# Delta attention and two Mlps in one kernel: two weight blocks converted later, and attention's list ordered by a table

## The chip, the cores and the metric

The kernel runs on one core of one Trainium2 chip. The metric is the device time of one execution in microseconds, the median of several; 1 us is 1000 ns. The engines are TensorE (PE in the rows; its weight loads are PEld), VectorE (DVE), ScalarE (ACT), GpSimd (POOL) and SyncE (SP), which issues most of the DMA transfers. Each engine works through its own instructions in the order in which the program lists them.

## The reference

Three stages, one after the other. Attention is a delta rule over 768 tokens for 32 (batch, head) pairs with 48 values each: a state that every token reads and updates. Its output, 3072 rows of 384, goes through two Mlps with 2048 hidden values; the first has a rational function between its two products, the second h * tanh(softplus(h)).

```python
for t in range(S):                       # 768 tokens, for all (batch, head) pairs
    y[:, :, t] = einsum('bhd,bhde->bhe', q[:, :, t], state)
    v_old = einsum('bhde,bhd->bhe', state, k_n[:, :, t])
    state = state + beta[:, :, t] * einsum('bhd,bhe->bhde', k_n[:, :, t], v[:, :, t] - v_old)

h = x @ moe_w_in                         # 3072 x 384 by 384 x 2048
g = (a0 + a1*h + a2*h**2 + a3*h**3) / (1 + |b0|*|h| + |b1|*h**2 + 1e-6)
x = g @ moe_w_out                        # 2048 x 384
h = x @ moe2_w_in
out = (h * tanh(log1p(exp(h)))) @ moe2_w_out
```

The weights of the Mlps come as 64-bit floats.

## The kernel before

**Attention** works in chunks of 64 tokens, twelve of them (u = 0 to 11), in class `Attention`. `prepare(u)` loads and normalizes k, transposes k and q on TensorE (line 383), copies them out on ScalarE (line 387), forms the Gram products (lines 398 and 419) and masks them on VectorE. `inverse(u)`, once for each pair of chunks, solves 32x32 triangular systems: a transpose on VectorE (line 534), then 30 short steps of a product and a sum each (lines 552 and 558) on GpSimd, or on VectorE for the pairs that end with u = 1 and u = 9 (`ON_DVE`), then a last product (line 580) and a transpose back into `xt` on VectorE (line 586). `step(u)` is the recurrence: products on TensorE (lines 690, 707, 728, 736 and 751), each evicted by ScalarE or VectorE before the next can start, from the state of chunk u to that of chunk u + 1. It needs the inverse of its pair (line 707 reads `xt`).

**The weights.** A product in full precision is made of three passes with a high and a low part of each operand, so each of the 16 blocks of 128 hidden values of each Mlp is converted from 64-bit floats first (class `Weights`). A block has two sides, w_in and w_out. One side is a raw load by SP, a scaling on ScalarE (`mag`, line 852), three bit operations on VectorE (`size`, `sign`, `low`; lines 856, 861, 867), a copy on ScalarE (`out`, line 874) and a difference on GpSimd (`rest`, line 879). All 16 blocks of the first Mlp are converted during attention: blocks 2 to 15 are stored to DRAM and fetched again when the first Mlp runs, blocks 0 and 1 stay. There the three bit operations keep their intermediate word in PSUM (`w1.word`); where that is not set, it lies in the raw block in SBUF.

**The order of attention.** `prepare`, `inverse`, `step`, the weights and the split of the first x group add every operation to a `Plan` with its engine, a duration written in the program, and the buffers that it reads and writes. `Plan.order` walks through time: whichever engine is free takes, of its operations that are ready, the one with the highest priority, which is the longest way to the end of the list (`tail`), less `early`, plus a bias of its kind (engine and first buffer written). For the weights `early` is 4000 ns times the block's place less 60000. `Plan.best` tries 2500 random changes of the biases and keeps those that don't lengthen the planned end; `Plan.run` issues the operations in that order and puts matmuls on zeros (`heat`, line 1239) into planned gaps of TensorE.

**The Mlps** run 96 units each: 6 groups of 512 tokens by 16 weight blocks. A unit is nine matmuls up (line 999), the function on ScalarE, VectorE and GpSimd, and nine matmuls down (line 1025) four units later. Each engine's order is written out in `MLP_OPS` and `FIRST_OPS` (the first four units). The up of unit i + 2 uses the PSUM bank that VectorE's second product of unit i (line 1090) frees. Ahead of unit 0 SP issues five weight fetches (`LOOK`, line 911), then one in each unit (`fw`).

**Conversions in the Mlps** go through class `Conv`: `start` issues three raw loads, `pull(n)` issues the next n of VectorE's steps and hands the ScalarE and GpSimd steps of a side to a list that the next unit's `f` empties; the first `mag` is issued at the first pull. Before, `Conv` holds the second Mlp's blocks alone. From unit `CONV_START` = 6 on, in units away from a new group (`calm`, 67 of them), it converts eight of them, 48 steps; the others in the second Mlp. In the list of a unit the pull, `c`, stands last.

```python
fetch_w = {n: (w1.fetch_split, FQ + LOOK + n) for n in range(NF - FQ - LOOK)}
calm = [i for i in range(CONV_START, n1 - 8) if not any(starts(i + 5 - k) for k in range(3))]
for f in range(LOOK):
    w1.fetch_split(FQ + f)
```

## Time and profile before

| what | us |
|---|---|
| median of 3 runs | 1092.06 |
| lowest and highest | 1089.65, 1092.43 |
| the profiled execution | 1098.82 |
| its span, first to last instruction | 1097.1 |
| TensorE busy in it | 1049.6 |
| VectorE, ScalarE, GpSimd busy | 686.7, 605.0, 553.0 |

The profile is one execution, and times in the rows are counted from the start of its span. An engine's busy time tells little by itself here, because matmuls on zeros count as busy. The views to read are the busy times by stage, the groups of instructions by line (with the idle time ahead of them and what ended it), and the instructions in order of time where one stage turns into the next. TensorE's granted clock stands in the windows as a share of 2.4 GHz.

### The profile page before, as it was taken

How to read it: one execution, taken by the hardware profiler on the slowest of the kernel's cores; microseconds unless marked ns; L12 is line 12 of the kernel's file. 1: busy time of each engine (PE TensorE's matmuls, PEld its weight loads, DVE VectorE, ACT ScalarE, POOL GpSimd, SP SyncE). 2: the span in 40 equal slices, each digit the busy share in tenths (PEclk: the TensorE clock that was granted, in tenths of full speed). 3: DMA queues.
4: the chain of work that ended last, by engine and by line, in shares of the span. 5: the costliest groups of instructions: out<-in, count | busy, mean ns of one | idle time of the engine just before them, and what ended most of it. 6: DMA issues, size and time to landing. Idle time of an engine off the chain costs nothing.

```text
span 1097.1 us, 24930 instructions
## 1 busy us (share of the span) xinstructions
PE 1049.6 (96%) x10228; PEld 895.5 (82%) x10228; DVE 686.7 (63%) x1154; ACT 605.0 (55%) x1081; POOL 553.0 (50%) x640
## 2 busy tenths in 40 slices
PE   7988889988889999999999999999999999999998
PEld 6988878877768888888888888888888888888897
DVE  6886658785369999999999999882222222222211
ACT  4534645324478888989889898643232322323222
POOL 4388998186268888787888888763000000000000
PEclk9998989889899999999999999999999999999999
DMA  8727875057691121211203046340101102011010
GB/s 127 139 63 182 223 201 138 10 152 218 220 362 70 39 78 43 84 47 73 87 15 104 13 144 245 101 145 1 28 30 15 43 2 57 1 22 36 10 20 29
DMA packets 152947, 99.25 MB, mean 90 GB/s; under 512 B 114048, under 2 KB 136192, under 8 KB 152832
## 3 DMA queue, kind: packets, MB, share of 16 engines
q1 hardware_dynamic: 150976, 96.77, 31.1%
q8 instruction: 80, 1.31, 0.5%
q10 hardware_dynamic: 1600, 0.79, 0.2%
q0 software_dynamic: 256, 0.10, 0.1%
q14 instruction: 35, 0.29, 0.1%
HBM read 66.16 MB, written 31.46 MB: 89 GB/s over the span
## 4 chain that ended last, share of the span: by engine, by line
PE 83%; DVE 7%; issue 3%; POOL 3%; ACT 1%; SPq 1%; DMA 1%; DVEq 0%; POOLq 0%; ACTq 0%
PE h L999 35%; PE o L1025 33%; PE o L1039 3%; PE c_ps L707 3%; PE y_ps L751 3%; DVE xraw L552 2%; PE c_ps L728 1%; PE c_ps L690 1%; PE t_ps L383 1%; SPq L252 1%; PE s_all L736 1%; DVE s_all L558 1%; POOL x L558 1%; PE t_ps L398 1%; DVE x L558 1%
## 5 line engine op out<-in xcount | busy, mean ns | idle before, releaser
L999 PE MATMUL h<-x,w 128*128 128x512 f32 x1728 | 426.4, 391 | 4.1 <-DVE s L1090 1.9
L1025 PE MATMUL o<-gh,w 128*128 128x512 f32 x1584 | 387.6, 389 | 0.0
L999 PEld LDWEIGHTS h<-x,w 128*128 128x128 f32 x1728 | 325.0, 188 | 73.8 <-DVE s L1090 3.0
L1025 PEld LDWEIGHTS o<-gh,w 128*128 128x128 f32 x1584 | 297.3, 188 | 61.7
L1121 ACT ACTIVATE gh<-h 128x512 fp32r<-128x512 f32 x96 | 57.5, 599 | 263.1 <-PE h L999 263.1
L1014 DVE TENSOR_TENSOR gh<-g,gh 128x512 fp32r<-128x512 f32 x80 | 55.0, 687 | 232.4 <-ACT g L1126 232.4
L1014 POOL TENSOR_TENSOR gh<-g,gh 128x512 fp32r<-128x512 f32 x112 | 145.4, 1299 | 67.4 <-ACT gh L1010 45.7
L1074 POOL TENSOR_TENSOR q<-q,r 128x512 f32<-128x512 f32 x96 | 131.8, 1373 | 29.9 <-ACT r L1068 25.1
L1088 DVE TENSOR_TENSOR s<-s,h 128x512 f32<-128x512 f32 x96 | 65.3, 681 | 27.7 <-ACT s L1070 17.0
L1070 ACT ACTIVATE s<-h,ab 128x512 f32<-128x512 f32 x96 | 74.0, 771 | 5.1 <-PE h L999 5.1
L1061 ACT ACTIVATE q<-h 128x512 f32<-128x512 f32 x96 | 57.5, 599 | 35.0 <-PE h L999 34.8
L1090 DVE SCALAR_TENSOR_TENSOR s<-s,ab,h 128x512 f32<-128x512 f32 x96 | 71.8, 748 | 3.4
L1101 DVE SCALAR_TENSOR_TENSOR r<-s,ab,r 128x512 f32<-128x512 f32 x96 | 71.8, 748 | 0.0
L1106 DVE SCALAR_TENSOR_TENSOR g<-q,r 128x512 f32<-128x512 f32 x96 | 66.0, 687 | 3.3
L1081 ACT ACTIVATE r<-q,cst 128x512 f32<-128x512 f32 x96 | 66.1, 688 | 1.7 <-POOL q L1074 1.7
L558 POOL TENSOR_TENSOR x<-x,xraw 128x30 f32<-128x30 f32 (+14 forms) x120 | 62.2, 518 | 9.4
L1097 DVE SCALAR_TENSOR_TENSOR q<-q,r 128x512 f32<-128x512 f32 x96 | 65.3, 680 | 0.9 <-ACT r L1083 0.6
L879 POOL TENSOR_TENSOR w<-wm,w 128x384 fp32r<-128x384 f32 x48 | 49.6, 1037 | 32.0 <-ACT w L874 23.7
L552 POOL TENSOR_TENSOR xraw<-x 128x30 f32<-128x30 f32 (+14 forms) x120 | 60.2, 502 | 7.3
L1010 ACT CAST gh<-g 128x512 fp32r<-128x512 f32 x96 | 59.1, 616 | 0.5 <-DVE g L1106 0.5
L1083 ACT ACTIVATE r<-r 128x512 f32<-128x512 f32 x96 | 55.9, 582 | 3.1
L1126 ACT ACTIVATE g<-h 128x512 f32<-128x512 f32 x96 | 57.0, 594 | 0.0
(139 smaller groups left out, 1283.5 us busy)
## 6 DMA issues: line engine op xcount, KB each, us to landing
w<-w SPq DMA_DIRECT2D x36, 768.0 KB, 6.9
w<-in_moe_w_in_dram SPq DMA_DIRECT2D x32, 384.0 KB, 3.7
w<-in_moe_w_out_dram SPq DMA_DIRECT2D x32, 384.0 KB, 3.6
xraw<-x SPq DMA_DIRECT2D x36, 256.0 KB, 4.1
w<-wt SPq DMA_DIRECT2D x8, 768.0 KB, 3.5
kn<-in_k_dram SPq DMA_DIRECT2D x48, 96.0 KB, 3.8
qn<-in_q_dram SPq DMA_DIRECT2D x48, 96.0 KB, 4.2
v<-in_v_dram SPq DMA_DIRECT2D x48, 96.0 KB, 3.4
```

The costliest lines, as they stand in the source:

```text
L552: eng.tensor_tensor(out=tv, in0=ls[:, j, j + 1:HC].unsqueeze(1).to_broadcast([128, j, n]), in1=xs[:, 0:j, j:j + 1].to_broadcast([128, j, n ...
L558: eng.tensor_tensor(out=xs[:, 0:j, j + 1:HC], in0=xs[:, 0:j, j + 1:HC], in1=tv, op=ALU.add)
L999: self.nc.tensor.matmul(out=self.st[i]["h"], lhsT=self.w.t[f][:, a, 0, k], rhs=self.x[g][:, b, k], start=(n == 0), stop=(n == 8),)
L1014: (nc.gpsimd if engine == "P" else nc.vector).tensor_tensor(out=s["gh"][:, 1], in0=s["g"], in1=s["gh"][:, 0].bitcast(F32), op=ALU.subtract)
L1025: self.nc.tensor.matmul(out=self.acc[g][d], lhsT=self.w.t[f][:, a, 1, d], rhs=self.st[i]["gh"][:, b], start=(first and n == 0), stop=(last ...
L1070: nc.scalar.activation(out=s["s"], in_=s["h"], func=ACTF.Identity, scale=k["a3"], bias=k["a2"])
L1074: nc.gpsimd.tensor_tensor(out=s["q"], in0=s["q"], in1=s["r"], op=ALU.mult)
L1081: nc.scalar.activation(out=s["r"], in_=s["q"], func=ACTF.Ln, bias=k["c"])
L1088: nc.vector.tensor_tensor(out=s["s"], in0=s["s"], in1=s["h"], op=ALU.mult)
L1090: nc.vector.scalar_tensor_tensor(out=s["s"], in0=s["s"], scalar=k["a1"], in1=s["h"], op0=ALU.add, op1=ALU.mult)
L1101: nc.vector.scalar_tensor_tensor(out=s["r"], in0=s["s"], scalar=k["a0"], in1=s["r"], op0=ALU.add, op1=ALU.mult)
L1106: nc.vector.scalar_tensor_tensor(out=s["g"], in0=s["q"], scalar=2.0, in1=s["r"], op0=ALU.subtract, op1=ALU.mult, reverse0=True)
```

## The change

Two things change.

The first Mlp's last two blocks, 14 and 15 (`DEFER`), leave attention's list. They are put at the head of `Conv`, whose raw loads are now issued right behind the five weight fetches and ahead of unit 0, and their twelve VectorE steps are pulled in units 0 to 10, about one a unit. They are not stored and not fetched; the tiles stay. `w1.word` is unset there, so the word lies in SBUF. The second Mlp's 48 steps follow from unit 11 on (`CONV_START`), in 62 calm units.

`Plan.best` is gone. `Plan.order` adds to each priority a number from the table `BIAS`, by the operation's kind, and another by its kind and the twelfth of the list in which it stands. The table has some 300 entries in ns, from -477472 to 406099; the walk through time is otherwise the old one, written with heaps.

In the diff lines with "..." are left out, most of them of the table.

```diff
--- before.py
+++ after.py
@@ -1,4 +1,4 @@
-import random
+import heapq
 from contextlib import ExitStack
 
 import concourse.bass as bass
@@ -25,6 +25,7 @@
 FQ = 2
 LOOK = 5
 DIRECT = 8
+DEFER = 2
 LOAD = 2700
 FIRST_PAIRS = (30000, 30000, 0)
 SETTLE = 6800
@@ -43,7 +44,64 @@
     "1a": 0, "1b": 0, "1c": 0, "1d": 0, "1e": 1, "1f": 1, "1g": 0, "1h": 0, "1i": 1, "1j": 1,
     "1k": 1, "1l": 2, "1m": 2, "2a": 1, "2b": 1, "2m": 1, "d": 4
 }
-CONV_START, CONV_RATE = 6, 4
+CONV_START, CONV_RATE = 11, 4
+
+
+BIAS = {
...
+    "ACT:nrm1s:3": -28213, "ACT:nrm1s:6": -10701, "ACT:s_ps": -196767, "ACT:s_ps:0": 68203, "ACT:w": -222613,
+    "ACT:w:10": 214086, "ACT:w:11": -268946, "ACT:w:9": -88442, "ACT:wm": -186276, "ACT:wm:10": 55109,
+    "ACT:wm:11": -51366, "ACT:wm:9": -2382, "ACT:x": 100641, "ACT:x1_": -51961, "ACT:x1_:9": 1023,
...
+    "DVE:wm:11": 99940, "DVE:wm:9": -315612, "DVE:word": -138883, "DVE:word:10": -73637, "DVE:word:11": -85758,
+    "DVE:word:9": 130084, "DVE:xs": -108267, "DVE:xs:1": 107871, "DVE:xs:2": -189779, "DVE:xs:4": -49217,
+    "DVE:xs:5": -29377, "DVE:xs:6": -101980, "DVE:xs:7": -70752, "DVE:xt": 11199, "DVE:xt:0": 235069,
+    "DVE:xt:1": 79946, "DVE:xt:3": 338907, "DVE:xt:4": -68512, "DVE:xt:6": 310548, "DVE:xt:7": -34745,
+    "DVE:xt:8": 90938, "DVE:yst": 38197, "DVE:yst:0": 142079, "PE:c": -25397, "PE:c:0": -275405, "PE:c:1": 4637,
...
+    "PE:s_ps:9": 46603, "PE:t": 229653, "PE:t:0": 25977, "PE:t:1": -180901, "PE:t:2": 95085, "PE:t:3": 60943,
+    "PE:t:4": 84259, "PE:t:5": 314698, "PE:t:6": 19231, "PE:t:7": -85083, "PE:y_ps": -1563, "PE:y_ps:2": 116447,
...
+    "POOL:w": -32381, "POOL:w:10": 382094, "POOL:w:11": -110467, "POOL:w:9": 37237, "POOL:x": 65037,
...
+    "POOL:xs:4": -27251, "POOL:xs:7": -47639, "POOL:xs:8": 57900, "SP:": 113757, "SP::0": 69170, "SP::10": -37718,
...
+    "SP:w": -36486, "SP:w:10": 261261, "SP:w:11": -205659, "SP:w:9": -37825, "SP:x1_": -49814, "SP:x1_:3": -151877,
...
+}
 
 
 class Ring:
@@ -98,69 +156,52 @@
         self.names.append(tuple(writes))
         self.ops.append((engine, ns, fn, sorted(need), more, early))
 
-    def order(self, bias=None):
-
-        n = len(self.ops)
-        tail, then, left = [0] * n, [[] for _ in range(n)], [0] * n
+    def order(self):
+
+        ops, n = self.ops, len(self.ops)
+        kinds = [f"{op[0]}:{names[0].strip('0123456789') if names else ''}" for op, names in zip(ops, self.names)]
+        tail, then = [0] * n, [[] for _ in range(n)]
         for i in range(n - 1, -1, -1):
-            engine, ns, fn, need, more, early = self.ops[i]
-            tail[i] += ns + more
-            left[i] = len(need)
-            for j in need:
+            tail[i] += ops[i][1] + ops[i][4]
+            for j in ops[i][3]:
                 then[j].append(i)
                 tail[j] = max(tail[j], tail[i] + self.HOP)
-        tail = [t - self.ops[i][5] + (bias or {}).get(self.kinds[i], 0) for i, t in enumerate(tail)]
-        ready = {}
+        rank = [
+            t - op[5] + BIAS.get(kind, 0) + BIAS.get(f"{kind}:{i * 12 // n}", 0)
+            for i, (t, op, kind) in enumerate(zip(tail, ops, kinds))
+        ]
+        engines = sorted({op[0] for op in ops})
+        left, at = [len(op[3]) for op in ops], [0] * n
+        later, now, free = ({e: [] for e in engines} for _ in range(3))
+        free = dict.fromkeys(engines, 0)
         for i in range(n):
             if not left[i]:
-                ready.setdefault(self.ops[i][0], []).append((0, i))
-        free, at, done = {}, [0] * n, []
-        while any(ready.values()):
-            best = None
-            for engine, queue in ready.items():
-                if queue:
-                    t = max(free.get(engine, 0), min(r for r, _ in queue))
-                    if best is None or t < best[0]:
-                        best = (t, engine)
-            t, engine = best
-            queue = ready[engine]
-            pick = max((x for x in queue if x[0] <= t), key=lambda x: (tail[x[1]], -x[1]))
-            queue.remove(pick)
-            i = pick[1]
-            end = t + self.ops[i][1]
-            free[engine] = end
+                heapq.heappush(later[ops[i][0]], (0, i))
+        done = []
+        while len(done) < n:
+            t, engine = min(
+                ((free[e] if now[e] else max(free[e], later[e][0][0]), e) for e in engines if now[e] or later[e]),
+                key=lambda x: x[0],
+            )
+            while later[engine] and later[engine][0][0] <= t:
+                i = heapq.heappop(later[engine])[1]
+                heapq.heappush(now[engine], (-rank[i], i))
+            i = heapq.heappop(now[engine])[1]
+            end = free[engine] = t + ops[i][1]
             done.append((t, end, i))
-            for j in then[i]:
+            for j in reversed(then[i]):
                 left[j] -= 1
-                at[j] = max(at[j], end + self.ops[i][4] + (0 if self.ops[j][0] == engine else self.HOP))
+                at[j] = max(at[j], end + ops[i][4] + (0 if ops[j][0] == engine else self.HOP))
                 if not left[j]:
-                    ready.setdefault(self.ops[j][0], []).append((at[j], j))
+                    heapq.heappush(later[ops[j][0]], (at[j], j))
         return done
 
-    TRIALS = 2500
-
-    def best(self):
-
-        def end(order):
-            return max(e for _, e, _ in order)
-        self.kinds = [(op[0], names[0].strip("0123456789") if names else "") for op, names in zip(self.ops, self.names)]
-        kinds, rng = sorted(set(self.kinds)), random.Random(0)
-        bias, order = {}, self.order()
-        for _ in range(self.TRIALS):
-            trial = dict(bias)
-            for k in rng.sample(kinds, rng.choice((1, 2, 4))):
-                trial[k] = trial.get(k, 0) + rng.gauss(0, rng.choice((1000, 5000, 20000)))
-            other = self.order(trial)
-            if end(other) <= end(order):
-                bias, order = trial, other
-        return order
-
     WINDOW, IDLE = 3400, 600
 
     def run(self, idle, unit):
 
         last, gaps, used = None, [], False
-        for t, end, i in self.best():
+        for t, end, i in self.order():
             engine, ns, fn = self.ops[i][:3]
             if engine == "PE":
                 if last is not None and t > last:
@@ -1178,7 +1219,10 @@
         for fn in fns:
             fn()
 
-    conv = Conv([w2.convert(f, side) for f in range(NF) for side in range(2)])
+    conv = Conv(
+        [w1.convert(f, side) for f in range(NF - DEFER, NF) for side in range(2)]
+        + [w2.convert(f, side) for f in range(NF) for side in range(2)]
+    )
 
     m1 = Mlp1(nc, w1, sb, ps, x1, consts)
     m2 = Mlp2(nc, w2, sb, ps, x2, consts)
@@ -1246,7 +1290,7 @@
         mctx.enter_context(tc.manual_schedule(engines=ALLE))
         plan = Plan()
         at.plan(plan)
-        w1.plan(plan, [*range(FQ, NF), *range(FQ)])
+        w1.plan(plan, [*range(FQ, NF - DEFER), *range(FQ)])
         late = 20000
         plan.add("SP", 300, fetch_ab, (), ["ab"], more=4000, early=late)
         plan.add("ACT", 250, lambda: nc.scalar.activation(out=ab[:, 4:6], in_=ab[:, 4:6], func=ACTF.Abs), (), ["ab"], early=late)
@@ -1266,12 +1310,14 @@
         ps2 = bctx.enter_context(tc.tile_pool(name="ps2", bufs=1, space=PSUM, reuse_waits="tile"))
         sb.add(sb2, w=16 - FQ, wt=1, w64=1, wm=1, x=1, q=3, s=3, r=2, g=3, gh=5, ev=3)
         ps.add(ps2, h=2, o=4, r=2)
-        fetch_w = {n: (w1.fetch_split, FQ + LOOK + n) for n in range(NF - FQ - LOOK)}
+        fetch_w = {n: (w1.fetch_split, FQ + LOOK + n) for n in range(NF - DEFER - FQ - LOOK)}
         for f in range(DIRECT):
             fetch_w[n1 - NF + 6 + f] = (w2.fetch_split, f)
         calm = [i for i in range(CONV_START, n1 - 8) if not any(starts(i + 5 - k) for k in range(3))]
         for f in range(LOOK):
             w1.fetch_split(FQ + f)
+        w1.word = None
+        conv.start()
         steps = [
             (m1, "1a", m1.e1, [0]), (m1, "1b", m1.e1, [1]), (m1, "1c", m1.e1, [2]), (m1, "1d", m1.e2, None),
             (m1, "1e", m1.e3, [0]), (m1, "1f", m1.e3, [1]), (m1, "1g", m1.e4, [0]), (m1, "1h", m1.e4, [1]),
@@ -1286,8 +1332,6 @@
         m2.pool = range(n1, n1 + NF)
         for i in range(n2 + max(LG.values())):
             kind = int(i >= n1)
-            if i == CONV_START - 3:
-                conv.start()
 
             def at_x(f):
                 for k in range(3):
@@ -1328,8 +1372,10 @@
                     w2.free = True
                     w2.word = w2.word or ps.tile([128, TOK], F32, "r")[:, 0:384]
                     conv.pull(CONV_RATE)
+                elif op == "c" and i < CONV_START:
+                    conv.pull(6 * DEFER * (i + 1) // CONV_START - conv.n)
                 elif op == "c" and i in calm:
-                    conv.pull(6 * DIRECT * (calm.index(i) + 1) // len(calm) - conv.n)
+                    conv.pull(6 * DEFER + 6 * DIRECT * (calm.index(i) + 1) // len(calm) - conv.n)
                 elif op == "f":
                     conv.flush()
     mctx.close()
```

## Rows read from the trace of the kernel before

**Rows 1.** Windows by stage: busy us per engine (instructions), clock, DMA share, GB/s

```profile
71.20:300.10 228.90, 197.91 (x5768) 181.46 (x5768) 155.72 (x293) 103.83 (x205) 156.74 (x253) 0.90 0.60 164
...
238.40:300.10 61.70, 52.83 (x1632) 49.81 (x1632) 31.74 (x56) 26.80 (x55) 29.00 (x44) 0.85 0.68 210
...
300.10:318.10 18.00, 13.93 (x45) 9.44 (x46) 8.41 (x13) 11.77 (x20) 10.72 (x10) 0.91 0.94 334
...
318.10:362.90 44.80, 44.80 (x199) 37.08 (x199) 41.86 (x64) 40.51 (x69) 37.24 (x31) 1.00 0.37 144
...
362.90:691.00 328.10, 328.10 (x1449) 271.67 (x1448) 306.21 (x463) 292.40 (x499) 267.35 (x222) 1.00 0.23 81
```

**Rows 2.** The chain of waits, 316 to 345 us: start us, us, what

```profile
320.34 2.04 PE h L999 x9
```

**Rows 3.** Page, groups: busy us, mean ns | idle us before, releaser

```profile
L999 PE MATMUL h<-x,w 128*128 128x512 f32 x1728 | 426.4, 391 | 4.1 <-DVE s L1090 1.9
```

**Rows 4.** Windows, line 1239 alone: PE, PEld, clock, DMA share, GB/s

```profile
71.20:300.10 228.90, 9.97 (x72) 9.02 (x72) 0.90 0.60 164
```

**Rows 5.** Windows of all engines, the two longest waits of the recurrence

```profile
183.00:198.00 15.00, 10.96 (x127) 9.42 (x126) 14.42 (x29) 2.46 (x5) 6.93 (x10) 0.92 0.15 28
...
230.60:238.40 7.80, 3.60 (x33) 3.41 (x31) 7.59 (x11) 0.00 (x0) 7.01 (x11) 0.89 0.48 105
```

**Rows 6.** Windows, line 1239 alone, the first of them

```profile
183.00:198.00 15.00, 6.34 (x42) 5.59 (x42) 0.92 0.15 28
```

**Rows 7.** Instructions in order of time, VectorE and GpSimd: start us, us, what

```profile
176.07 2.01 DVE L534 STREAM_TRANSPOSE x<-lg 128x1024 f32<-128x1024 f32 x1 [0.43 <-ACT lg L466]
...
188.80 1.91 POOL L580 TENSOR_TENSOR x<-x 128x1024 f32<-128x1024 f32 x1
...
194.90 1.97 DVE L586 STREAM_TRANSPOSE xt<-x 128x1024 f32<-128x1024 f32 x1
...
236.40 1.94 DVE L586 STREAM_TRANSPOSE xt<-x 128x1024 f32<-128x1024 f32 x1
```

**Rows 8.** Windows, line 879 alone: GpSimd busy, clock, DMA, GB/s

```profile
238.40:300.10 61.70, 13.10 (x14) 0.85 0.68 210
```

**Rows 9.** Groups of instructions, VectorE, 0 to 302.5 us: the conversion in attention

```profile
L861 DVE SCALAR_TENSOR_TENSOR word<-wm,word 128x384 int32<-128x384 int32 x32 | 17.9, 561 | 0.9
...
L856 DVE TENSOR_SCALAR word<-wm 128x384 int32<-128x384 int32 x32 | 17.8, 555 | 19.6 <-ACT wm L852 18.7
...
L867 DVE SCALAR_TENSOR_TENSOR wm<-w,word 128x384 int32<-128x384 int32 x32 | 17.7, 553 | 2.2
```

**Rows 10.** Groups, 330 to 690 us, and one line's instructions (ns min/median/max)

```profile
L867 DVE SCALAR_TENSOR_TENSOR wm<-w 128x384 int32<-128x384 int32 x16 | 11.7, 729 | 0.0
...
L856 DVE TENSOR_SCALAR w<-wm 128x384 int32<-128x384 int32 x16 | 11.0, 687 | 0.0
...
L861 DVE SCALAR_TENSOR_TENSOR w<-wm,w 128x384 int32<-128x384 int32 x16 | 10.8, 674 | 0.0
...
L856 DVE TENSOR_SCALAR w<-wm x16: 353/654/1197, 335.8 to 654.0; 128x384 int32<-128x384 int32 x16
```

**Rows 11.** Instructions in order of time, VectorE and TensorE: the lead of unit 6

```profile
322.43 0.75 DVE L1090 SCALAR_TENSOR_TENSOR s<-s,ab,h 128x512 f32<-128x512 f32 x1
...
324.26 2.20 PE L999 MATMUL h<-x,w 128*128 128x512 f32 x9
```

**Rows 12.** Instructions in order of time, the junction: SP, ScalarE, TensorE

```profile
307.01 0.90 SPq L911 DMA_DIRECT2D w<-w  x2
...
307.90 0.82 ACT L1068 ACTIVATE r<-q,ab 128x512 f32<-128x512 f32 x1
...
312.37 2.34 PE L999 MATMUL h<-x,w 128*128 128x512 f32 x9 [0.59 <-DVE s L1090]
```

**Rows 13.** DMA issues: KB each, us to landing; page, then 285 to 345 us

```profile
w<-in_moe_w_in_dram SPq DMA_DIRECT2D x32, 384.0 KB, 3.7
...
w<-in_moe_w_in_dram SPq DMA_DIRECT2D x3, 384.0 KB, 10.0
```

40 rows, old and new, of the table BIAS are left out of this document.

## The prediction

> **What bounds the kernel now.** The windows by stage come first [rows 1]: the reader should see a start up to 71.2 us, an attention recurrence from 71.2 to 300.1, a short junction up to 318.1, and then two stages in which TensorE is busy all the time. In those the chain of waits goes through TensorE alone, nine matmuls in 2.04 us for an up and, in the piece that follows each such piece, as much for a down, so one unit takes 4.08 us [rows 2], and the groups of costliest instructions show that the ups waited 4.1 us in the whole run [rows 3]. From 318.1 us on, then, nothing can be won, only lost: the end moves with the instant at which TensorE becomes dense, and the change acts ahead of it.
>
> Attention is the loose part. Between 71.2 and 300.1 us TensorE was busy 197.91 of 228.9 us [rows 1], but 9.97 us of that were matmuls on zeros that only keep it warm [rows 4]. So 228.9 - (197.91 - 9.97) = 41.0 us did no work. The mean granted clock there is 0.90 [rows 1], a mixture of its two levels (2.4 and 1.2 GHz), worth another 0.10 x 228.9 = 23 us. No engine beside TensorE is near full: VectorE stands at 155.72 and GpSimd at 156.74 of the 228.9 us [rows 1]. What ends last is a chain across engines, and the order of the list sets how long it waits. About 64 us is the most that any order could give back; a quarter to a half of such a sum is already much, since each product of the recurrence waits for the eviction of the one before it, whatever the order.
>
> Two places show how it waits. Between 183 and 198 us TensorE was busy 10.96 us [rows 5], 6.34 of them on zeros [rows 6], so 15 - (10.96 - 6.34) = 10.4 us without work; between 230.6 and 238.4 us all of the 7.8 us. In both the recurrence waits for a 32x32 inverse. GpSimd's last product of pair (6,7) ran from 188.80 to 190.71 us, yet VectorE's transpose of it began only at 194.90, 4.2 us later, behind steps of another inverse in VectorE's queue; and that other pair, (8,9), took VectorE from 176.07 to 238.34 us, because it shares the engine with everything else [rows 7]. The last stretch, 238.4 to 300.1 us, has no inverse on VectorE any more, but 14 of the 32 weight sides [rows 8], 8.9 us of idle TensorE and a clock of 0.85 (another 9.3 us) [rows 1].
>
> **The change, part by part.** (1) Two of sixteen weight blocks leave attention: 4 of 32 sides. Each is one ScalarE step before and one after three VectorE steps of 555, 561 and 553 ns [rows 9], so VectorE loses 4 x 1.67 = 6.7 us, GpSimd about 4 x 0.94 = 3.7 us [rows 8], and SP four raw loads and two stores. Most of this is beside the chain. Where it counts is the last stretch: 4 of 14 sides, and 4/14 of its 18.2 us of idle and slow clock is 5.2 us at the most, nothing at the least. I take 2.5, the middle, since the steps there sit between the evictions of the recurrence on in-order queues.
>
> (2) The table replaces the search over 2500 trials by fixed priorities per kind of step and per twelfth of the list. Read by hand it does three things that bear on the rows above. The weight steps on VectorE get priorities between about -9,000 and -790,000 ns and those on ScalarE between about -8,000 and -490,000, where the old rule left them a positive rank that beat the recurrence in the last tens of microseconds; so they become filler. VectorE's final transposes (kind xt) rise in all twelfths but two, by 11,000 to 350,000. TensorE's transposes and Gram products (kind t) rise by 49,000 to 544,000, so an inverse can start earlier. The first answers the last stretch, the second the 4.2 us, the third the two long waits. The trace cannot show the new order, so I bound it: a loss of 2 us (an order may also push an inverse back; the nearest row is the 7.8 us wait, and a quarter of it is my lower end) to a gain of 30 us (a little under half of 64). I take half of the two long waits, (10.4 + 7.8) / 2 = 9.1, a little over a fifth of the 15.7 us that (1) leaves of the last stretch's 18.2, 3.5, because ten of its sides must still be done somewhere, and 1 us of clock after the long waits: 13.6. With (1) attention ends 16 us earlier, bounds 2 later to 32 earlier.
>
> (3) The four sides come back in units 0 to 10 of the first Mlp. TensorE isn't touched, and the ScalarE and GpSimd steps lie beside other work (40.51 and 37.24 of 44.8 us; but see 4), but VectorE is nearly full: 41.86 of 44.8 us over 318.1 to 362.9 [rows 1], with three of the old conversion's steps in it. There the same three steps average 687, 674 and 729 ns [rows 10], so twelve are 8.4 us; less the three that leave units 6 to 10 (2.1), 6.3 come against 2.9 us that were free. The lead that hides them is small: the second product of unit 4 ended at 323.18 us, and the matmuls of unit 6, which need its bank, began at 324.26 [rows 11]. Of the overrun of 3.4 us that lead hides 1.1 at the most and the gaps behind unit 10 some more; against it, unit 3 waits for VectorE already, 0.59 us [rows 12]. I take half, 1.7 us; with no lead left it is 3.4.
>
> (4) The wait added: ScalarE's first conversion step stands at the end of unit 0's steps, and its raw block is loaded by SP behind five weight fetches. The fifth of them was issued at 307.01 us, behind the landing of attention's last store, whose space it fills [rows 12]. The raw load would follow half a microsecond later. ScalarE is through with unit 0 at 308.72 [rows 12] and then stands until the block lands; queued behind it are unit 1's two evictions, and VectorE's products, and TensorE's unit 3 wait for those. The nearest rows for the landing are 3.7 us (the median of the run) and 10.0 us (the same load while the queue was full) [rows 13]. One fetch of 768 KB ahead of it is nearer the first: landing at about 311.5, a wait of 2.8 us (2.5 to 8.8). Parts (3) and (4) together: +4.5 us, bounds +1 (SP is let go earlier, the block lands in time and VectorE's idle start takes the steps) and +10.5 (8.8 + 1.7). No gain can come here: what leaves the junction, two fetches, TensorE does not wait for.
>
> (5) The second Mlp's 48 conversion steps move from 67 units to 62, 0.774 a unit instead of 0.716. VectorE was busy 306.21 of 328.1 us there [rows 1]; 0.058 x 0.7 = 0.04 us a unit fits in the 0.27 us that are free. Zero; if that cover were gone, 62 x 0.04 = 2.5 us.
>
> The sum: -16 + 4.5 = -11.5 us. The profiled execution lasted 1098.82 us (its span 1097.1 and 1.7 around it) and would become 1087.3; the median of the runs shown is 1092.06, 6.8 us below it, and the same step gives 1080.6.
>
> **A rule against part (3).** The trace shows the size step at 353 to 1197 ns in the first Mlp, with one operand layout [rows 10], where attention has 555 ns in the mean with the word in PSUM [rows 9]. The Trainium skill, page "SBUF — State Buffer", section "Who interferes with whom", says that a VectorE instruction with two SBUF inputs, or in a two-port mode, and a GpSimd instruction that reads SBUF block one another for a whole instruction; the spread agrees. By that rule alone every one of the twelve steps could stand behind a GpSimd step. By the rows, twelve steps at 1197 instead of 697 ns are 6.0 us more: 1086.6.
>
> **The rivals.** *More comes back than a half:* both long waits vanish and the clock stays up in the last stretch, attention -30, junction +3: 1065. For it: VectorE and GpSimd are below 70% in attention. Against: outside the two waits and the last stretch, 41.0 - 10.4 - 7.8 - 8.9 = 13.9 us lie scattered over the other 144 us, and no single order closes them.
> *The order doesn't carry over:* the list is ordered by durations written in the program, not by the chip's waits, or the table's keys do not hit what they should, and new waits take the old ones' place. Only part (1) and a little remain, -4, and +4.5 in the junction: 1092.6, no change. For it: the old order too was searched on those durations, and it still left 41 us without work.
> *ScalarE stands at the junction (slower):* the raw block lands as the loads did in the full queue, 10.0 us after its issue. ScalarE then stands 8.8 us, TensorE waits for unit 3, and the junction costs 10.5. It decides against the change as soon as attention gives back less than 10.5 - 3.3 = 7 us; with 5 it is 1097.6. For it: the DMA share was 0.94 in the junction [rows 1]. Against: the queue ahead of that block is shorter than it was.
> *VectorE blocked step by step,* as worked out above: 1086.6.
>
> **How the numbers follow.** The likeliest 0.47 (1080.6, own range 1072 to 1088), more back 0.17, the order doesn't carry over 0.15, ScalarE stands 0.13, VectorE blocked 0.08. About 0.3%, 3.3 us, is what a measurement of this kernel can tell from no change, so faster is below 1088.8 and slower above 1095.3. Faster: 0.46 + 0.17 + 0.01 + 0.06 = 0.70; slower: 0.04 + 0.12 = 0.16; the same: the rest, 0.14. Half of the case at 1065 lies below 1064 and most of the slower one above 1096; together they are under 0.2, so the range is 1064 to 1096.
>
> **What the profile after would show.** Right: the last small matmul of attention at about 284 us; the transposes behind an inverse within a microsecond of it; the clock above 0.90 in the recurrence; ScalarE idle 2 to 4 us before its first conversion step, ended by a load; ups waiting some 4 us more than now. Wrong: two waits of over 5 us for an inverse still there, or weight steps crowded behind the last step of attention (the order didn't carry over); waits for VectorE beyond unit 10 (parts 3 and 5 under-priced).

## The result, and the profile after

The changed kernel is **slower by 0.9%**: 1101.97 us, the median of 16 runs, against 1092.24 for the kernel before in 16 runs beside them. The ratio is 1.0091, with a 95% interval of 1.0067 to 1.0114. One of the 16 runs, 1111.20 us, is over 1.5% above the fastest of its kernel and is left out of the ratio. The forecast was 1080.6 in a range from 1064 to 1096.

The profiled execution after lasted 1101.58 us (span 1099.8), that of before 1098.82, some 6.6 above the median of its kernel. So the kernel before was profiled once more (`b2`), 1095.36 us. Stage by stage, in us of each profile; attention ends with the last small product into `y`, the junction reaches from there to the first down of the first Mlp, and the tail from there to the end:

| kernel | attention ends | junction | tail | span |
|---|---|---|---|---|
| before, the profile shown | 300.06 | 18.1 | 779.0 | 1097.1 |
| before again (`b2`) | 295.64 | 19.0 | 778.9 | 1093.6 |
| after | 295.09 | 23.0 | 781.7 | 1099.8 |

Two things are to be read here. Attention is not shorter than in an ordinary execution of the kernel before, and the junction and the tail are longer, by 4 to 5 and 2.8 us. The windows by stage of after (busy us of PE, PEld, VectorE, ScalarE, GpSimd, then the granted clock, DMA share, GB/s) answer to [rows 1]:

```profile
71.20:300.10 228.90, 192.28 (x5758) 176.39 (x5757) 148.32 (x280) 102.85 (x201) 158.37 (x253) 0.92 0.59 156
300.10:318.10 18.00, 13.69 (x41) 9.99 (x41) 9.37 (x15) 10.71 (x18) 6.48 (x6) 0.75 0.80 287
318.10:362.90 44.80, 43.46 (x188) 34.67 (x187) 44.03 (x64) 39.49 (x69) 37.26 (x33) 1.00 0.34 124
362.90:691.00 328.10, 328.10 (x1450) 271.72 (x1449) 313.43 (x470) 293.86 (x501) 269.14 (x223) 1.00 0.23 82
```

The clock in the junction is 0.75, where it was 0.91, and in the 44.8 us behind it TensorE is no longer busy throughout: 1.34 us are missing, with VectorE at 44.03 of 44.80. Over the last stretch, where the second Mlp's conversion runs in fewer units, TensorE is still busy all the time. The page's group of the ups shows the same loss, 7.9 us idle where [rows 3] had 4.1:

```profile
L1040 PE MATMUL h<-x,w 128*128 128x512 f32 x1728 | 429.6, 393 | 7.9 <-DVE s L1131 5.7
```

**The junction.** The chain of waits of after runs through the load that the prediction named (start us, us, what):

```profile
293.48 9.72 DMA x<-yst
303.28 5.36 DMA w<-in_moe_w_in_dram
308.66 0.54 ACT wm L893
```

And in order of time on SP, ScalarE, VectorE and TensorE (in brackets the idle time ahead and what ended it):

```profile
290.23 12.75 SPq L952 DMA_DIRECT2D w<-w  x5
303.28 0.38 SPq L882 DMA_DIRECT2D w<-in_moe_w_in_dram  x1
...
308.66 0.54 ACT L893 ACTIVATE wm<-w 128x384 f32<-128x384 f32 x1 [4.77 <-DMA w<-in_moe_w_in_dram]
...
309.23 0.36 DVE L897 TENSOR_SCALAR w<-wm 128x384 int32<-128x384 int32 x1 [4.68 <-ACT wm L893]
...
311.91 3.58 PE L1040 MATMUL h<-x,w 128*128 128x512 f32 x9 [4.05 <-DVE s L1131]
315.75 2.51 PE L1040 MATMUL h<-x,w 128*128 128x512 f32 x9 [0.26 <-DVE s L1131]
...
354.92 2.34 PE L1040 MATMUL h<-x,w 128*128 128x512 f32 x9 [1.19 <-DVE s L1131]
```

The fifth of SP's fetches waits for attention's last stores to land, the first late raw block goes out right behind the landing of the second of them (293.48 + 9.72 = 303.20) and lands 5.36 us later, and ScalarE stands 4.77 us with unit 1 queued behind it. TensorE then waits 4.05 us for unit 3, where [rows 12] had 0.59, and the nine matmuls that follow take 3.58 us, where the same nine took 2.34: 1.24 us more, at the lower clock. The last line is a wait for VectorE well behind the junction.

**The inverses.** VectorE's final transposes (into `xt`), as in [rows 7], with GpSimd's last products of pairs (4,5) and (6,7) ahead of them, and then GpSimd's conversion steps in the stretches between them (windows of that line alone: busy us and count, clock, DMA share, GB/s):

```profile
138.53 1.91 POOL L621 TENSOR_TENSOR x<-x 128x1024 f32<-128x1024 f32 x1
...
140.80 2.00 DVE L575 STREAM_TRANSPOSE x<-xraw 128x1024 f32<-128x1024 f32 x1
142.71 2.00 DVE L627 STREAM_TRANSPOSE xt<-x 128x1024 f32<-128x1024 f32 x1
...
194.71 1.98 POOL L621 TENSOR_TENSOR x<-x 128x1024 f32<-128x1024 f32 x1
...
199.66 1.91 DVE L627 STREAM_TRANSPOSE xt<-x 128x1024 f32<-128x1024 f32 x1
...
239.97 1.95 DVE L627 STREAM_TRANSPOSE xt<-x 128x1024 f32<-128x1024 f32 x1
```

```profile
88.00:143.00 55.00, 11.14 (x12) 0.88 0.80 211
143.00:200.00 57.00, 7.12 (x7) 0.91 0.69 172
```

The same window of the kernel before, up to its own transpose, with that transpose and the product ahead of it:

```profile
88.00:139.00 51.00, 8.24 (x9) 0.91 0.81 219
...
136.75 1.91 POOL L580 TENSOR_TENSOR x<-x 128x1024 f32<-128x1024 f32 x1
...
138.69 2.03 DVE L586 STREAM_TRANSPOSE xt<-x 128x1024 f32<-128x1024 f32 x1 [1.12 <-POOL x L580]
```

The transposes start at 199.66 and 239.97 us, where they started at 194.90 and 236.40 [rows 7]. Pair (6,7) waits less between its last product (GpSimd, to 196.69) and its transpose, 3.0 us for 4.2, but the product itself is 5.9 us later. At pair (4,5) the product ends at 140.44, and the transpose stands 2.3 us behind it: VectorE takes the first transpose of another inverse (`x<-xraw`) before it. TensorE's two long waits are still there (windows of all engines, then line 1283 alone, the matmuls on zeros):

```profile
183.00:202.00 19.00, 12.31 (x202) 11.00 (x198) 17.71 (x32) 4.94 (x11) 14.52 (x22) 0.91 0.36 104
233.00:242.00 9.00, 4.54 (x44) 4.35 (x41) 8.69 (x13) 0.00 (x0) 7.98 (x14) 0.95 0.36 70
```

```profile
183.00:202.00 19.00, 4.49 (x34) 4.02 (x34) 0.91 0.36 104
233.00:242.00 9.00, 4.51 (x38) 4.32 (x38) 0.95 0.36 70
```

Without work were 19 - (12.31 - 4.49) = 11.2 and 9 - (4.54 - 4.51) = 9.0 us, where the same reckoning gave 10.4 and 7.8 in windows of 15 and 7.8 us. Only the last stretch gained: from the first product behind the wait, at 241.97, to the end 53.1 us, where `b2` took 58.2 (237.44 to 295.64). The wait ahead of it ends 4.5 us later than in `b2`, so in this pair of profiles the gain of 5.1 pays for the late inverses and for little more.

### The profile page after: what moved, and what is told of

Its sections match the earlier page's. It is cut to its first block, busy times and chain, and to the rows that moved or that the text cites. A ratio compares the mean times of both kernels' runs of the same rounds, so it can differ in the third digit from the quotient of the medians.

```text
span 1099.8 us, 24890 instructions
## 1 busy us (share of the span) xinstructions
PE 1044.6 (95%) x10216; PEld 889.9 (81%) x10216; DVE 692.5 (63%) x1154; ACT 605.5 (55%) x1081; POOL 553.2 (50%) x640
## 4 chain that ended last, share of the span: by engine, by line
PE 72%; DVE 4%; POOL 4%; DMA 3%; ACT 3%; issue 2%; ACTq 0%; SPq 0%; DVEq 0%; POOLq 0%
PE h L1040 33%; PE o L1066 31%; PE o L1080 3%; DMA x<-yst 2%; PE y_ps L792 1%; POOL x L599 1%; POOL xraw L593 1%; PE c_ps L748 1%; PE t_ps L439 1%; PE c_ps L769 1%; DMA w<-in_moe_w_out_dram 1%; DMA w<-in_moe_w_in_dram 0%; DVE x L599 0%; DVE r L739 0%; PE c_ps L731 0%
## 5 line engine op out<-in xcount | busy, mean ns | idle before, releaser
L1055 POOL TENSOR_TENSOR gh<-g,gh 128x512 fp32r<-128x512 f32 x112 | 147.7, 1320 | 71.2 <-ACT gh L1051 49.4
```

The source lines that it names most:

```text
L1055: (nc.gpsimd if engine == "P" else nc.vector).tensor_tensor(out=s["gh"][:, 1], in0=s["g"], in1=s["gh"][:, 0].bitcast(F32), op=ALU.subtract)
```

## The experiments

Ratios are to the kernel before in runs on the same chip, with their 95% intervals; stages come from each kernel's own profile. They tell apart three things: what the table's order gave, what the late steps cost, and in which of two ways the late steps cost it: ScalarE standing behind the raw block (J1 for short) or VectorE having no room (J2).

**The two halves of the change.** `e1_table_only` converts all sixteen blocks in attention under the table; `e2_defer_only` defers two and orders the list by the old search.

```diff
# e1, against after
-        w1.plan(plan, [*range(FQ, NF - DEFER), *range(FQ)])
+        w1.plan(plan, [*range(FQ, NF), *range(FQ)])
...
# e2, against before (Plan.best stays)
-        w1.plan(plan, [*range(FQ, NF), *range(FQ)])
+        w1.plan(plan, [*range(FQ, NF - DEFER), *range(FQ)])
...
```

> The table's order with all sixteen blocks converted in attention, and the Mlps as they were; no late steps. Two theories. J, the late steps at the junction cost the time: the order itself gives back what the two profiles show for attention, 5.0 us (its last small matmul ended at 295.1 instead of 300.1 us), less about 1.5 for the four sides that come back: 1087 to 1090 where the kernel before has 1092. O, the order is no better on the chip than the searched one, or worse: 1092 to 1100.

> The searched order of the kernel before (it searches again, over a list with four sides fewer), and blocks 14 and 15 converted in units 0 to 10. J: the junction and the units behind it cost 8 us or more, attention gets perhaps 2 us shorter: 1098 or above. O: the deferral is a small part of the loss: 1092 to 1096.

Measured: e1 1.0069 [1.0040, 1.0098], attention 304.95; e2 1.0091 [1.0055, 1.0127], attention 300.93, junction 21.7. Neither half is faster than before. In e1 the first up waits for the conversion of its own block, which the table leaves too late (it was likely made for a list of 28 sides; no run shows that this is why):

```profile
311.23 6.10 PE L1040 MATMUL h<-x,w 128*128 128x512 f32 x18 [6.29 <-DVE wm L908]
```

**The late steps left out.** `e4_no_late_steps` keeps the table and the 28 sides; `e7_searched_no_late` does the same under the old search. Both leave out the raw loads and the steps of blocks 14 and 15, whose units read the tiles of blocks 12 and 13.

```diff
# e4, against after
...
+            if i == NF - DEFER:
+                w1.t[14], w1.t[15] = w1.t[12], w1.t[13]
...
-                elif op == "c" and i < CONV_START:
-                    conv.pull(6 * DEFER * (i + 1) // CONV_START - conv.n)
```

> The changed kernel without any conversion of blocks 14 and 15: units of these blocks read the tiles of blocks 12 and 13 instead, so that part of the first Mlp's output is another one; everything else stands. J: all that the late steps cost goes, 8 us by the two profiles, and with the shorter attention it comes under the kernel before: about 1087 to 1090, 12 or more below the changed kernel. O: attention is not shorter in most executions, and it comes out at 1092 to 1096.

> The searched order over 28 sides and no late steps: blocks 14 and 15 read the tiles of 12 and 13, so that part of the first Mlp's output is another one. Beside the run without late steps under the table's order (0.999 of the kernel before) it shows the order alone at equal work. If the table's order is worth what those two profiles show (attention's end at 294.8 against 300.9 us), this comes out 5 to 7 us above it, 1098 to 1101. If it is worth nothing in most executions, both are the same within 3 us.

Measured: e4 0.9990 [0.9968, 1.0011], attention 294.82, junction 16.4, tail 779.2; e7 1.0097 [1.0070, 1.0124], attention 299.24, junction 17.6, tail 779.3. After and e4 end attention within 0.3 us of one another, so the late steps cost (23.0 - 16.4) + (781.7 - 779.2) = 9.1 us by the stages, and 1.0091 - 0.9990 = 1.01%, 11 us (within some 3.5), by the ratios. Not all of the 9.1 is theirs: the first three units, ahead of ScalarE's stand, took 12.0 us in after at a mean granted clock of 0.72, 10.2 in e4 at 1.00, and 11.7 at 0.71 in `b2`, which has no late steps (windows of all engines: after, e4, `b2`):

```profile
295.85:307.86 12.01, 10.51 (x27) 7.07 (x27) 1.44 (x2) 3.55 (x6) 5.02 (x4) 0.72 0.92 299
...
295.58:305.80 10.22, 7.89 (x28) 5.22 (x29) 3.14 (x5) 6.01 (x10) 6.64 (x6) 1.00 0.88 280
...
296.40:308.06 11.66, 10.45 (x27) 6.97 (x27) 2.13 (x3) 5.52 (x10) 5.65 (x5) 0.71 0.97 345
```

So 1.8 us of the 9.1 may be of the two executions and not of the late steps. The order and the four sides fewer together gave 0.1%, about 1 us (between 3.5 gained and 1.2 lost). At equal work the table is 1.1% better than this search; but e7 does less work than the kernel before and is 1% slower, so what it is compared with there is a bad draw of the search. e2 beside e7, the late steps under the searched order, shows no cost in the ratios (1.0091 and 1.0097), though its junction is 4.1 and its tail 1.3 us longer. Both rest on six runs; taken together their intervals leave room for a cost of 4 us at the most, less than under the table, and why is open.

**How much a draw of the search is worth.** `e10_other_seed` is the kernel before with another seed, all operations the same; `b2_before_again` is the kernel before itself.

```diff
-        kinds, rng = sorted(set(self.kinds)), random.Random(0)
+        kinds, rng = sorted(set(self.kinds)), random.Random(1)
```

> The kernel before with another seed for its search over the order (1, not 0); every operation is the same. L, what an order that is short on the planned durations is worth on the chip is luck of several us: it differs from the kernel before by 3 us or more, more likely slower, 1095 to 1103. M, the planned end carries over: within 3 us of it, and then the table's gain has to be looked for elsewhere.

> The kernel before once more, unchanged, for a second profile of it: the one shown lasted 1098.8 us, 6 us more than its median, and its attention ended at 300.1 us. V: that was a late end of attention, and an ordinary execution ends it at 294 to 296 with the same 18 us of junction. W: attention's end is steady within 1 us, as it was over three profiles with the table and 28 sides (294.8 to 296.1), and the spread of the runs lies elsewhere: 300 again.

Measured: e10 1.0028 [1.0001, 1.0054]; b2 1.0017 [0.9990, 1.0044]. The other seed is 3 us slower by the ratio, and its interval just excludes no change; e7's search, over a shorter list, came out 1% slower. That the old order was itself a lucky draw is likely by these two, not shown.

**ScalarE or VectorE.** `e3_raw_ahead` issues the first raw load ahead of the five fetches; `e5_later_pulls` leaves the loads and pulls the steps in units 3 to 12.

```diff
+        conv.sides[0][0]()                                     # e3, ahead of the LOOK fetches
...
-        conv.start()
+        for side in conv.sides[1:3]:
+            side[0]()
...
-CONV_START, CONV_RATE = 11, 4
+CONV_START, CONV_RATE = 13, 4                                  # e5
...
-                    conv.pull(6 * DEFER * (i + 1) // CONV_START - conv.n)
+                    conv.pull(max(0, 6 * DEFER * (i - 2) // (CONV_START - 3)) - conv.n)
```

> The changed kernel with one line moved: the raw load of the first late side is issued ahead of the five weight fetches, not behind them; the two others stay. J: ScalarE's 4.8 us wait for that load goes, and with it the 4.1 us that TensorE waits for unit 3 and its slow clock after that: 5 to 6 us less than the changed kernel, about 1096. O: the wait is hidden in other waits of the start: less than 2 us, 1100 or above.

> The changed kernel with the twelve late VectorE steps in units 3 to 12, not 0 to 10, so that the first ScalarE step waits for a load that has long landed; the second Mlp's steps start at unit 13. J1, ScalarE's stand at the junction is the loss: its 4.8 us and the slow clock behind it go, 5 to 7 us less than the changed kernel, 1095 to 1097 where that has 1102. J2, VectorE's steps are the loss: at most 2 us less, and the waits for VectorE grow behind unit 5.

Measured: e3 1.0057 [1.0035, 1.0080], junction 23.5; e5 1.0068 [1.0042, 1.0094], junction 17.8, tail 783.9. In e3 the stand was not removed but moved, one side on; the first step now goes at once, and the second side's raw block, issued at 309.35, is the late one:

```profile
304.37 0.54 ACT L893 ACTIVATE wm<-w 128x384 f32<-128x384 f32 x1
...
312.33 0.54 ACT L893 ACTIVATE wm<-w 128x384 f32<-128x384 f32 x1 [4.30 <-DMA w<-in_moe_w_out_dram]
...
315.59 4.21 PE L1040 MATMUL h<-x,w 128*128 128x512 f32 x9 [4.84 <-DVE s L1131]
```

So the run does not test what the stand costs; its ratio lies a little under that of after, with intervals that overlap. In e5 the junction is 5.2 us shorter. Of these 0.9 us are the first three units, at a clock of 0.85 where after had 0.72. The other 4.3 us are ScalarE's stand: TensorE's wait for unit 3 is 0.37 us, not 4.05, and the nine matmuls behind it take 2.33 us at a clock of 1.00, not 3.58 at 0.61 (the wait in e5, then windows of all engines over the nine matmuls in after and over both stretches in e5):

```profile
307.26 2.33 PE L1040 MATMUL h<-x,w 128*128 128x512 f32 x9 [0.37 <-DVE s L1131]
...
311.91:315.49 3.58, 3.58 (x9) 2.33 (x9) 3.51 (x6) 3.55 (x7) 1.22 (x2) 0.61 0.96 398
...
295.77:306.89 11.12, 9.49 (x27) 6.06 (x27) 2.56 (x4) 5.97 (x10) 6.03 (x6) 0.85 0.97 299
307.26:309.59 2.33, 2.33 (x9) 1.61 (x9) 2.29 (x4) 2.30 (x5) 0.69 (x1) 1.00 1.07 387
```

But VectorE, crowded into fewer units, is now late further on, and the tail gives 2.2 us back:

```profile
314.29 0.56 ACT L893 ACTIVATE wm<-w 128x384 f32<-128x384 f32 x1
...
354.17 2.35 PE L1040 MATMUL h<-x,w 128*128 128x512 f32 x9 [1.74 <-DVE s L1131]
...
360.16 2.33 PE L1040 MATMUL h<-x,w 128*128 128x512 f32 x9 [1.61 <-DVE s L1131]
```

Both ways are real, then: J1 costs after's junction some 4.3 us, and J2 shows as 1.34 us of waits in after and 3.4 in e5, most of it around the units in which VectorE also prepares the next group's input.

**The sides split.** `e9_sides_split` converts the four sides w_in first and leaves those units free; `e11_split_sooner` is through with the last side one unit sooner.

```diff
-CONV_START, CONV_RATE = 11, 4
+CONV_START, CONV_RATE = 18, 4
+LATE_UNITS = [*range(3, 11), *range(14, 18)]                  # e9; e11: 2 to 10 and 14 to 16
...
-        [w1.convert(f, side) for f in range(NF - DEFER, NF) for side in range(2)]
+        [w1.convert(f, side) for side in range(2) for f in range(NF - DEFER, NF)]
...
-                    conv.pull(6 * DEFER * (i + 1) // CONV_START - conv.n)
+                    conv.pull(int(i in LATE_UNITS))
```

> The changed kernel with the late steps one a unit in units 3 to 10 and 14 to 17, the w_in sides of both blocks first, so that none of them stands in units 11 to 13, where VectorE splits the next x group; the second Mlp's steps from unit 18 on. The run with units 3 to 12 had a junction of 17.8 us, as short as before, but 783.9 us behind the first down where the kernel before has 778.9, in waits for VectorE around 354 and 360 us. J2, VectorE's load in units 11 to 15 is the rest of the loss: those waits go, 780 to 781 behind the first down, 1094 to 1096. Otherwise the waits move to other units and it stays at 1098.

> The four late sides w_in first, as in the split before, but one step a unit in units 2 to 10 and 14 to 16, so that the last side is through one unit (4.08 us) sooner. In the split before, TensorE waited 0.31 us for ScalarE's copy and 1.40 us for GpSimd's rest of the last side at the down that reads it (370.5 to 372.4 us), 1.7 us in all. Theory (that wait is the side's lateness): it goes, the stretch from the first down on takes 780.0 us instead of 781.8, and the ratio to before is 1.0012. Rival 1 (the first step in unit 2 is ahead of its raw block, issued at 298.5 us and 5.6 us under way): ScalarE or VectorE stands in the junction again by up to 2 us, TensorE waits for unit 4 or 5, the clock falls, and the ratio stays at 1.0028 or rises to 1.005. Rival 2 (twelve steps cost what they cost): the wait comes back as one for VectorE in units 14 to 16, ratio 1.0028.

Measured: e9 1.0028 [1.0000, 1.0057], junction 17.7, tail 781.8; e11 1.0008 [0.9984, 1.0032], junction 18.9, tail 780.3. In e9 the waits for VectorE behind the junction are gone, but a down waits for the last side itself:

```profile
370.52 0.50 PE L1067 MATMUL o<-gh,w 128*128 128x512 f32 x1 [0.31 <-ACT w L916]
...
372.42 2.14 PE L1067 MATMUL o<-gh,w 128*128 128x512 f32 x8 [1.40 <-POOL w L921]
```

e11 takes that wait away too, and its tail is 1.5 us shorter. The step from e9 to e11 is seen in the profiles; in the ratios it is smaller than their intervals. From 1.0091 to 1.0008 by the order and the place of the twelve steps: the change's loss lies in where they stood. No version here is faster than the kernel before.

**What paces the inverses.** `e6_rests_last` takes GpSimd's conversion steps, whose priority the table had raised by 349,713 ns (-32381 + 382094) in the part of the list with key 10, below everything else; `e8_rests_between` goes part of the way, on top of e5.

```diff
-    "POOL:w": -32381, "POOL:w:10": 382094, "POOL:w:11": -110467, "POOL:w:9": 37237, ...
+    "POOL:w": -900000, "POOL:w:10": 0, "POOL:w:11": 0, "POOL:w:9": 0, ...         # e6
+    "POOL:w": -32381, "POOL:w:10": 132094, "POOL:w:11": -110467, ...              # e8
```

> The changed kernel with the priority of GpSimd's weight step (kind w) at -900000 in all parts of the list, so that it never goes ahead of a step of an inverse. P, these steps pace the inverses: 12 of them (11.1 us) lie between the inverses of pairs (2,3) and (4,5) and 7 (7.1 us) before that of (6,7), whose transposes began at 142.7 and 199.7; the first comes 5 to 9 us earlier, the second 8 to 14, and attention ends 5 or more earlier, 1096 or below. Q, the inverses are paced by VectorE and the recurrence: the transposes come within 3 us of where they were, and the conversions, held up, crowd behind attention: 1102 or above.

> The changed kernel with the late steps in units 3 to 12, and GpSimd's weight step in the eleventh part of the list at 132094 instead of 382094: between the changed kernel, where it goes ahead of the inverses, and the run with it behind them, whose inverses came 13 and 16 us earlier, whose attention ended 6.5 us earlier, and where the ups then waited 39.9 us for the conversions. T, the two trade evenly: what the inverses gain the conversions lose, attention's last small matmul 1 to 4 us earlier than 295.0 and some waiting for conversions behind it, 1095 to 1105. If the conversions fit without crowding: 1093 or below, which would beat both kernels. If they crowd as before: 1110 or above.

Measured: e6 1.0359 [1.0330, 1.0389]; e8 1.0063 [1.0041, 1.0084]. In e6 the three transposes above start 13.1, 16.5 and 8.5 us sooner and attention ends 6.5 us sooner, at 288.54, but fourteen of the sides are then finished behind it (VectorE's last bit step in the 40 us behind attention, windows of that line alone, and then the first up):

```profile
129.60 2.02 DVE L627 STREAM_TRANSPOSE xt<-x 128x1024 f32<-128x1024 f32 x1 [3.49 <-POOL x L621]
...
183.19 1.96 DVE L627 STREAM_TRANSPOSE xt<-x 128x1024 f32<-128x1024 f32 x1 [4.14 <-POOL x L621]
```

```profile
288.50:328.50 40.00, 7.77 (x14) 0.54 0.80 272
...
328.48 6.29 PE L1040 MATMUL h<-x,w 128*128 128x512 f32 x18 [39.93 <-DVE wm L908]
```

e8 lies between: attention ends at 291.97, and the first up waits 5.74 us for a weight; against e5 nothing is won. How much of its 3 us is the order cannot be told, since executions of one and the same attention list scatter as far: with the table and 28 sides it ended at 295.09, 296.10, 294.82, 295.01, 291.01 and 295.31 us (after, e3, e4, e5, e9, e11). e6's 288.54 and its transposes lie outside that. GpSimd does both, the products of the inverses and the conversion's last step, and taking all of the latter back makes the conversions late instead. Their number alone does not set an inverse's time, though. Under e7's searched order five of them stand ahead of pair (4,5), and its transpose starts as late as in after (windows of that line alone, then VectorE):

```profile
88.00:142.60 54.60, 5.02 (x5) 0.87 0.65 160
...
142.66 2.01 DVE L587 STREAM_TRANSPOSE xt<-x 128x1024 f32<-128x1024 f32 x1
```

In e2, with the same list, it is 143.66 behind five, in e10 139.98 behind eleven.

## Why the prediction was wrong

The forecast was 21.4 us below the median measured. Two parts make that up, 15 of it in steps (1) and (2) and 6.5 in steps (3) and (4).

**Steps (1) and (2), attention 16 us earlier: wrong, and the larger error.** e4 has both and none of the later cost, and gave 1 us. The share of the four sides alone was not measured; both are bounded by that sum. The step that failed was "I take half of the two long waits", 9.1 us: the waits are there as before, 11.2 and 9.0 us, and the second ends 4.5 us later than in `b2`. The 6 us taken for the last stretch nearly came, 5.1 against `b2`, and the late inverses used them up. The signs in the table were read for VectorE, ScalarE and TensorE, and the transposes were raised indeed, but a transpose can only follow its inverse, and 2.3 and 3.0 us still lie between the two for pairs (4,5) and (6,7). GpSimd's conversion steps had been raised as well, to 12 in 11.14 us ahead of the inverse that is transposed at 142.71, where the kernel before had 9 in 8.24 us, and the reading left that entry out. One of the 12 ran from 141.2 us, behind the inverse's last product, so 11 stand ahead of that product, against 9. The late inverse is no accident of one execution: in after, e4, e5, e9 and e11 that transpose starts between 141.6 and 143.7 us, in the two profiles of before at 138.7 and 138.3. That taking the conversion's last steps away brings the inverses forward is shown by e6. That two more of them, some 2 us, made this inverse late is not shown, and e2 and e7, as late with five, speak against their number alone. Of the 4.0 us between 138.7 and 142.71, GpSimd's product explains 1.8 (it ended at 140.44, in the kernel before at 138.66), and VectorE's other transpose, taken first, most of the rest. What holds the product back under the table stays open. The lower bound, a loss of 2 for the order with nothing from the sides, would have covered what came; the value taken was far from it.

A second weakness lies under it. The 41.0 us without work were read from an execution whose attention ended at 300.06; `b2` ended at 295.64 with the same instructions. So some 4 us were likely of that execution, not of the kernel, and the sum carried a gain from a late profile over to a median.

**Step (4), ScalarE's wait: right in its mechanism and place, undersized.** SP issued the load at 303.28, 8.2 us behind the end of attention (307.01 + 0.5 against 300.06, so 7.5, in the forecast), the landing took 5.36 us, between the rows' 3.7 and 10.0, and ScalarE stood 4.77 us where 2.8 was taken. What the step left out is that such a wait costs twice: TensorE stood 4.05 us, and ran its next nine matmuls at a clock of 0.61, 1.24 us longer.

**Step (3), VectorE's room: right in kind, undersized as well.** The twelve steps took 10.5 us, 0.88 each, where 0.70 was taken. TensorE's later waits of 1.19 and 0.15 us are near the 1.7 forecast, but e4 to after the tail lost 2.5. The stretch in which VectorE also prepares the next group's input (units 11 to 13) was not looked at; e5 and e9 show that it is the tight one. Together (3) and (4) cost 9.1 by the stages, 1.8 of it perhaps the clock of the first units, and 11 by the ratios, against 4.5 taken and a bound of 10.5.

The rule set against this part is borne out in part. Of four steps of one form two took 1.66 us, the others 1.07 and 0.83, and in each case GpSimd was within an instruction when the step began (VectorE's steps, then the GpSimd instructions under the first three):

```profile
317.59 1.07 DVE L908 SCALAR_TENSOR_TENSOR wm<-w 128x384 int32<-128x384 int32 x1
...
329.41 1.66 DVE L908 SCALAR_TENSOR_TENSOR wm<-w 128x384 int32<-128x384 int32 x1
...
342.75 0.83 DVE L908 SCALAR_TENSOR_TENSOR wm<-w 128x384 int32<-128x384 int32 x1
...
351.83 1.66 DVE L908 SCALAR_TENSOR_TENSOR wm<-w 128x384 int32<-128x384 int32 x1
```

```profile
317.48 0.78 POOL L1105 TENSOR_SCALAR r<-q,ab 128x512 f32<-128x512 f32 x1
...
329.37 1.29 POOL L1115 TENSOR_TENSOR q<-q,r 128x512 f32<-128x512 f32 x1
...
341.87 1.30 POOL L1115 TENSOR_TENSOR q<-q,r 128x512 f32<-128x512 f32 x1
```

Each step ended 0.4 us behind GpSimd's instruction: at 318.66, 331.07 and 343.58, where that ended at 318.26, 330.66 and 343.17. The Trainium skill, page "SBUF — State Buffer", section "Who interferes with whom", says that a VectorE instruction with two SBUF inputs contends with a GpSimd instruction that reads SBUF; the trace agrees for these steps, which read both of their inputs from SBUF. But a step waits only for what is left of GpSimd's instruction, 0.7, 1.2 and 0.4 us here, and so the mean of twelve, 0.88 us, lies between the 0.70 taken and the 1.20 of that rival.

**Step (5), zero: right.** TensorE was busy 328.10 of 328.1 us, and e4, with the 62 units, has a tail of 779.2 us against 779.0 and 778.9 before.

**The rivals.** What came was two of them at once: the order didn't carry over, and ScalarE stood at the junction. The second was said to decide as soon as attention gives back less than 7 us; it gave 1. They were priced one at a time, 1092.6 and 1097.6, each with part of the gain of (1) and (2) left in it. With 1 us from attention the second comes to 1092 - 1 + 10.5 = 1101.5. That this meets the measured 1101.97 is in part luck: its 10.5 has a stand of 8.8 us in it, and 4.77 was measured. Of the marks named, the two waits of over 5 us for an inverse, and waits for VectorE beyond unit 10, were the ones that showed.

## What to carry to other kernels

Raising the step that takes a result over gains nothing while the result itself is late: before a wait is booked as a gain, ask which engine makes the awaited result, and what else is queued on that engine and on the one that takes it over. Work put at the head of a dense stage needs its data loaded before that stage, and a place in units whose engines have room; here the place of twelve short steps decided 0.8% of the run. Take a stage's length from two profiles of the same kernel before a gain is built on it.

## What was not expected of the hardware

Two profiles of one kernel differ by 4.4 us in a single stage (300.06 and 295.64) and by nothing in the dense one (779.0 and 778.9): the spread of the runs, 1087.04 to 1096.93 in these 16, is consistent with one that arises where engines wait for one another. And both gaps of 4 to 5 us among the ups were followed by slow matmuls: nine took 3.58 us behind 4.05 (after), and 4.21 behind 4.84 (e3), where nine took 2.33 to 2.35 us behind waits of 1.19 to 1.74 us (after and e5, further on). Not only long waits go with a lower clock, though: in e2 nine took 3.30 us behind 1.97, and the first three units ran at 0.71 to 1.00 in executions in which no wait among them was over 0.83 us.
